# Reordering a weight conversion and two sets of channel sums in a fused attention and MLP kernel

## The chip, the cores and the metric

The kernel runs on one core of one Trainium2 chip. The metric is the device time of one execution in microseconds (us), the median of several runs. The engines of the core are TensorE (PE in the profile, its weight loads PEld), VectorE (DVE), ScalarE (ACT), GpSimd (POOL) and SyncE (SP, which here only issues DMAs). Each works through its own instructions in order and waits for others by semaphores.

## The reference

```python
def _attn_ref(q, k, v, S1, S2):                      # q, k, v: (4, 4, 1088, 32), S1, S2: (8, 32)
    def phi(x):
        a = np.einsum('rd,bhsd->bhsr', S1, x)
        b = np.einsum('rd,bhsd->bhsr', S2, x)
        return np.einsum('bhsi,bhsj->bhsij', a, b).reshape(*x.shape[:-1], r * r)
    q_p, k_p = (phi(q), phi(k))
    kv = np.einsum('bhsf,bhsd->bhfd', k_p, v)
    z = np.sum(k_p, axis=2)
    num = np.einsum('bhsf,bhfd->bhsd', q_p, kv)
    den = np.einsum('bhsf,bhf->bhs', q_p, z)[..., None] + 1e-06
    return num / den

# x: (4352, 128) = attention output as tokens by channels; w_in (128, 2048), w_out (2048, 128)
h = x @ w_in
g = 0.5 * h * (1.0 + erf(h / sqrt(2)))
out = g @ w_out
```

A linear attention with features of 64 values for each head is followed by an MLP with an exact gelu. S1, S2, w_in and w_out arrive as 64-bit floating-point numbers, and the engines work on 32-bit ones, so the kernel converts them itself.

## The kernel before

**Tiles and steps.** The 4352 tokens are cut into eight chunks of 512 and a ninth of the remaining 256. The hidden width of 2048 is cut into 16 tiles of 128 (`NF`). A step `t` is one pair (chunk, tile): `hidden` multiplies the weight tile by the chunk's tokens into PSUM (L740, two matmul passes) and ACT takes the gelu (L747). The steps go: t = 0 to 3 are tiles 0 to 3 of chunk 0, t = 4 to 11 tiles 0 to 7 of chunk 1, t = 12 to 23 the rest of chunk 0, t = 24 to 31 the rest of chunk 1, and then chunk after chunk.

**Two ways to multiply by w_out.** The first four tiles of chunk 0 and the first eight of chunk 1 are multiplied directly (`project`, L925). All others go by a scheme of seven products in place of eight. Four hidden tiles make a block (`NB`). For each block POOL forms four sums of gelu results, `token_sums` (L791 to L794, into the tiles bits_low, bits_a, bits_e and bits_m, four operations on 128x512), right after the block's last gelu. For each piece of w_out POOL once forms four sums of weights, `channel_sums` (L778 to L781, into the `small` tiles). `two_products` (L826) multiplies them on PE some steps later. The first products of a block are "4" and "7", which need the channel sums of the piece and the block's first token sum, bits_low. Block 1 of chunk 0 (t = 12 to 15) uses piece 2 of w_out, block 2 (t = 16 to 19) piece 3, block 3 (t = 20 to 23) piece 4. The products of block 1 begin in step 19, those of block 2 in step 22, those of block 3 in step 26.

**The weight pieces.** w_in and w_out are cut into five pieces each, two of 256 and three of 512. Pieces 0 and 1 are converted before the steps and in the first of them. Pieces 2, 3 and 4 are the six "turns", in the order w_in 2, w_out 2, w_in 3, w_out 3, w_in 4, w_out 4. A conversion (`Rounding`) of one piece has seven operations on 128x512:

- on DVE by `begin`: the exponent field (L283) and the mantissa field (L288);
- on ACT by `by_scalar`: the low words (`low_words`, L270) and the exponents (`exponents`, L294, which needs L283);
- on DVE by `end`: mantissas (L302, needs the low words), signs (L307, needs the exponents), and the product that writes the weights (L312). For some pieces the product goes to POOL instead (`multiply`).

`begin` of a turn stands ahead of `end` of the turn before it, so DVE's order is fields of the next piece, then mantissas, signs and product of this one.

**Order.** `at(t, f, ...)` puts a function in the list `slots[t]`. In a step the loop issues `hidden`, then the token sums, then the functions of the slot in the order in which `at` named them, then the products. In step 4, `first_hidden` and the products stand ahead of `hidden`. At the end every engine's instructions are tied to the order of the text, so no scheduler moves them.

**What follows the turns.** At t = 13 DVE turns the keys of batch 1 (`key_turn_blocks`, L383, two tiles kT), at t = 15 the queries of chunk 2 (L554). At t = 16 PE multiplies the turned keys (`features_of_all`, L1043, sixteen small matmuls, eight for each kT), then turns the remaining keys (L348); at t = 17 it uses those (L421). DVE makes features of the keys (L1051 to L1058) and sums them over tokens (L1067). On POOL, `widen_v_rem` (L364, L366) copies the remaining values of batch 1 when they have landed.

The SP queue issues all loads and most stores; the loads of the pieces, then of the later batches, are issued in one list before the steps.

Of the kernel before, what the change touches and what calls it, by code (L numbers as in the profile page):

```python
# [16 lines left out]
def kernel(  # L17
# [18 lines left out]
    pe, dve, act, pool, sp = nc.tensor, nc.vector, nc.scalar, nc.gpsimd, nc.sync  # L36
# [31 lines left out]
    def work_banks():  # L68

        return wps.tile([128, 2, CW], FP, name="w_ps")  # L70

    def work_bank():
        return work_banks()[:, 0]

    def halves(banks):
        return [banks[:, i] for i in range(2)]

    def hidden_bank():
        return hps.tile([128, CW], FP, name="h_ps")
# [494 lines left out]
    def expand_copy(n, i):  # L574
        A[i] = att.tile([128, 2, CW // 2], FP, name="A_sb")
        act.copy(out=A[i][:, :, :width[n] // 2], in_=B_of[n, i][:, :, :width[n] // 2])

    def expand_multiply(n, i):
        W = width[n]
        a, b = (t.rearrange("f g (r x) -> f g r x", r=2) for t in (A[i][:, :, :W // 2], B_of[n, i][:, :, W // 2:W]))  # L580
        dve.tensor_mul(out=qp[n].rearrange("f r (g x) -> f g r x", g=G)[:, 2 * i:2 * i + 2], in0=a, in1=b)
# [96 lines left out]
    def numerators_by_token(n, banks, tokens):  # L678

        for at, i in enumerate(tokens):  # L680
            to = by_head(banks[at // 2]).rearrange("p (j c r) x -> p j r c x", j=2, c=NP)[:, at % 2]
            for r in range(2):
                for half in range(2):
                    rows, tok = slice(half * 64, (half + 1) * 64), i * 128 + half * 64
                    pe.matmul(to[rows, r], lhsT=qp[n][:, r, tok:tok + 64], rhs=kz_apart[:, r], start=True, stop=True)
# [5 lines left out]
    def divide(n, banks, first, den=None):  # L691

        if den is None:
            den = att.tile([128, NP, 2 * H], FP, name="den_tok")
            for i, bank in enumerate(banks):
                dve.tensor_scalar(out=den[:, i], in0=by_head(bank)[:, :, D], scalar1=1e-6, scalar2=None, op0=AX.add)
        den = den[:, :len(banks)]
        dve.reciprocal(out=den, in_=den)
        for i, bank in enumerate(banks):
            dve.tensor_mul(out=x_half(n, first + i).rearrange("p j h d -> p (j h) d"), in0=by_head(bank)[:, :, 0:D],  # L700
                           in1=den[:, i, :, None].broadcast_to([128, 2 * H, D]))
# [25 lines left out]
    def w_tile(w, fi):  # L727
        i = max(i for i, (c0, c1) in enumerate(pieces) if c0 <= fi * 128)
        at = fi * 128 - CUTS[i]
        return w[i][:, at:at + 128]  # L730
# [3 lines left out]
    def hidden(n, fi, by_halves=False):  # L734
        W = width[n]
        ps = first_banks.pop((n, fi)) if (n, fi) in first_banks else hidden_bank()
        w = w_tile(w_in_sb, fi)
        for rows in (slice(0, 64), slice(64, 128)) if by_halves else (slice(0, 128),):
            if (n, fi) not in begun:
                pe.matmul(ps[rows, :W], lhsT=w[:, rows], rhs=xT[n][:, :W], start=True, stop=True)  # L740
        if n < NCH and fi < USUAL[n]:
            g_of[n, fi] = mlp.tile([128, CW], FP, name="g", bufs=4)
        else:
            if fi % NB == 0:
                blocks[n, fi // NB] = block(FP)
            g_of[n, fi] = blocks[n, fi // NB][:, fi % NB]
        act.activation(out=g_of[n, fi][:, :W], in_=ps[:, :W], func=ACT.Gelu)  # L747

    def first_hidden(n, half):

        if half == 0:
            first_banks[n, 0] = hidden_bank()
        parts = 1 if n else 2
        for i in range(parts):
            cols = slice(half * 256 + i * 256 // parts, half * 256 + (i + 1) * 256 // parts)
            pe.matmul(first_banks[n, 0][:, cols], lhsT=w_tile(w_in_sb, 0), rhs=xT[n][:, cols], start=True, stop=True)  # L756
# [53 lines left out]
    def first_block(n):  # L810
        return USUAL[n] // NB if n < NCH else 0
# [102 lines left out]
    def project(n, fi, parts=range(B // 2), cols=slice(None)):  # L914
        first, final = fi == (BLOCKED if n == NMAIN else 0), fi == (USUAL[n] if n < NCH else NF) - 1
        if first and n not in o_of:
            o_of[n] = out_bank() if n < NMAIN else [out_bank() for i in range(B // 2)]
        g = g_of[n, fi]
        if n == NMAIN:

            for i in parts:
                pe.matmul(o_of[n][i][:, :128], lhsT=g[:, i * 128:(i + 1) * 128], rhs=w_tile(w_out_sb, fi),  # L922
                          start=first, stop=final)
            return
        pe.matmul(o_of[n][:, cols], lhsT=w_tile(w_out_sb, fi), rhs=g[:, cols], start=first, stop=final)  # L925
# [107 lines left out]
    def at(t, f, *a):  # L1033
        slots[t].append(lambda: f(*a))
# [90 lines left out]
    def begin(w):  # L1125

        rounding[w.name] = Rounding(w)
        rounding[w.name].fields()

    def by_scalar(w, *what):  # L1130
        for f in what:
            getattr(rounding[w.name], f)()
# [10 lines left out]

    turns = [w[i] for i in range(2, 5) for w in (w_in_sb, w_out_sb)]
    both, low, exp = ("low_words", "exponents"), ("low_words",), ("exponents",)
    at(4, begin, turns[0])
    for k, acts in enumerate((((4, both),), ((5, low), (6, exp)), ((7, both),), ((8, low), (9, exp)), ((10, both),),
                              ((11, low), (12, exp)))):
        if k + 1 < len(turns):
            at(acts[-1][0], begin, turns[k + 1])  # L1150
        for t, what in acts:
            at(t, by_scalar, turns[k], *what)
        at(acts[-1][0], end, turns[k], dve if k < 4 else pool)
    at(12, channel_sums, 3)
    at(12, widen_v_rem, 1)
    at(12, multiply, turns[4])
    at(13, multiply, turns[5])
    for r in range(2):
        at(13, key_turn_blocks, 1, r)
    at(15, query_turn, 2)  # L1160
# [11 lines left out]
    at(24, query_sketch, 2)  # L1172
    at(26, lambda: turn_kv(1, held["kv"]))
    at(24, query_outer, 2)
    for i, t in enumerate((5, 6, 8)):
        at(t, channel_sums, i)
    at(6, spread_sketches)
    at(40, repeat_first_z)
    for n in range(3, NCHUNK):

        t = (n - 1) * NF
# [75 lines left out]
    for t in range(len(steps) + LAG):  # L1257
        if t < 4:

            hidden(0, t)  # L1260
            if t == 0:
                expand_multiply(1, 0)
                w_out[0].fields()
                expand_copy(1, 1)
                expand_multiply(1, 1)
            if t == 1:
                w_out[0].low_words()
                w_out[0].exponents()
                w_out[0].finish()
                w_out[1].fields()  # L1270
            if t == 2:
                w_out[1].low_words()
            if t == 3:
                banks = work_banks()
                numerators_by_token(1, halves(banks), range(JC))
                w_out[1].mantissas(by_pool=True)
                w_out[1].exponents()
                divide(1, halves(banks), 0)
                w_out[1].signs()
                w_out[1].product()  # L1280
                project(0, 0)
                project(0, 1, cols=slice(0, 256))
                turn_half(1, 0, work_bank(), by_act)
                project(0, 1, cols=slice(256, 512))
                turn_half(1, 1, work_bank(), by_dve)
            continue
        if t == 4:
            first_hidden(1, 0)
            for f, *a in products[t]:
                f(*a)  # L1290
            first_hidden(1, 1)
        for n in drains[t]:
            drain(n)
        sooner = t == NMAIN * NF
        if sooner:
            for f, *a in products[t]:
                f(*a)
        if t < len(steps):
            n, fi = steps[t]
            hidden(n, fi, by_halves=t >= 18)  # L1300
        if t < len(steps) and steps[t][0] < NMAIN and steps[t][1] % NB == NB - 1:
            n, b = steps[t][0], steps[t][1] // NB
            if b >= first_block(n):
                token_sums(n, b)
        for f in slots[t]:
            f()
        for n in done[t]:
            store(n)
        if t != 4 and not sooner:
            for f, *a in products[t]:  # L1310
                f(*a)
# [41 lines left out]
```

## Time and profile before

| | |
|---|---|
| runs | 258.88, 258.69, 258.60 us; median 258.69 |
| profiled execution | 258.58 us, its span 256.7 us |
| PE | 252.0 us busy (98% of the span), granted clock 1.00 |
| DVE | 158.1 us busy (62%) |
| ACT | 114.2 us busy (44%) |
| POOL | 180.1 us busy (70%) |
| chain that ended last | PE 91%, DVE 6%, issue 1%, ACT 1% |

The profile is of one execution. The span runs from its first to its last instruction, and all positions below are microseconds from the span's start. A row of a timeline gives start, length, engine, line, operation, tiles and shapes, and in brackets how long the engine was idle before it and which instruction ended that. Rows of one engine overlap slightly, as instructions are pipelined; the distance from start to start is what an instruction costs its engine. The chain that ended last is followed back from the last instruction: at each step to what released it.

### The profile page before, as it was taken

Reading aid. Unit: us, or ns where it says so; the run is one execution under the profiler, and the core shown is the slowest. Engines: PE = TensorE matmul, PEld = TensorE weight load, DVE = VectorE, ACT = ScalarE, POOL = GpSimd, SP = SyncE. Lnnn points to the kernel's source line nnn. Section 1 sums busy time; section 2 is a strip of 40 time slices with the busy share of each in tenths; the row PEclk is TensorE's granted clock in tenths of the full one; section 3 lists DMA queues with packets and bytes.
Section 4 is the critical chain, followed back from the end, with each engine's and each line's share of the span. In section 5 each row is a group of like instructions: output and inputs, shape, how many; then the busy total and the mean of one; then the engine's idle time right before and its main releaser. Section 6 shows DMA issues by size and latency. Waiting matters only on the chain.

```text
span 256.7 us, 5996 instructions
## 1 busy us (share of the span) xinstructions
PE 252.0 (98%) x2427; PEld 132.8 (52%) x2427; DVE 158.1 (62%) x330; ACT 114.2 (44%) x221; POOL 180.1 (70%) x195
## 2 busy tenths in 40 slices
PE   8999999999999999999999999999999999999995
PEld 4755443455444545444444455455444444445784
DVE  4898999939798996580178986399307000700382
ACT  3784883433535333533335332533444333533541
POOL 3419548996858777587758775787758777877950
PEclk9999999999999999999999999999999999999999
DMA  6689558710001101102000002000200200020021
GB/s 209 201 284 315 150 117 217 195 18 8 0 3 15 26 4 20 23 10 33 3 0 0 0 13 35 0 4 0 40 4 4 40 1 3 5 36 3 0 35 31
DMA packets 29083, 13.50 MB, mean 53 GB/s; under 512 B 21888, under 2 KB 27264, under 8 KB 29056
## 3 DMA queue, kind: packets, MB, share of 16 engines
q1 hardware_dynamic: 28624, 12.79, 20.1%
q8 instruction: 19, 0.31, 0.5%
q10 hardware_dynamic: 432, 0.33, 0.4%
q14 instruction: 8, 0.07, 0.1%
HBM read 10.88 MB, written 2.23 MB: 51 GB/s over the span
## 4 chain that ended last, share of the span: by engine, by line
PE 91%; DVE 6%; issue 1%; ACT 1%; POOL 0%; DVEq 0%; ACTq 0%
PE h_ps L740 41%; PE o_ps L826 35%; DVE bits_e L307 2%; PE w_ps L896 2%; PE w_ps L456 1%; DVE bits_m L302 1%; PE w_ps L604 1%; PE w_ps L659 1%; PE w_ps L957 1%; PE o_ps L925 1%; PE w_ps L570 1%; PE w_ps L1043 1%; PE o_ps L922 1%; PE h_ps L756 1%; DVE bits_a L288 1%; PE h_ps L348 1%
## 5 line engine op out<-in xcount | busy, mean ns | idle before, releaser
L740 PE MATMUL h_ps<-xT,w_in 128*64 128x512 f32 (+2 forms) x536 | 137.2, 567 | 0.0
L747 ACT ACTIVATE block<-h_ps 128x512 f32<-128x512 f32 (+1 forms) x132 | 75.4, 572 | 119.1 <-PE h_ps L740 117.2
L826 PE MATMUL o_ps<-block,w_out 128*64 128x256 f32 x232 | 59.5, 379 | 0.0
L791 POOL TENSOR_TENSOR bits_low<-block 128x512 f32<-128x512 f32 x29 | 37.2, 1283 | 29.2 <-ACT block L747 29.2
L740 PEld LDWEIGHTS h_ps<-xT,w_in 128*64 128x64 f32 (+1 forms) x536 | 40.9, 140 | 26.9 <-issue 8.7
L826 PEld LDWEIGHTS o_ps<-block,w_out 128*64 128x64 f32 x232 | 31.7, 137 | 39.2 <-issue 28.3
L792 POOL TENSOR_TENSOR bits_a<-block 128x512 f32<-128x512 f32 x29 | 37.0, 1276 | 12.5 <-ACT block L747 12.5
L841 DVE COPY sums<-o_ps 64x256 f32<-64x256 f32 x8 | 3.3, 417 | 60.2 <-PE o_ps L826 60.2
L793 POOL TENSOR_TENSOR bits_e<-bits_a,block 128x512 f32<-128x512 f32 x29 | 37.3, 1288 | 2.3
L794 POOL TENSOR_TENSOR bits_m<-block,bits_e 128x512 f32<-128x512 f32 x29 | 37.1, 1279 | 2.3
L826 PE MATMUL o_ps<-block,small 128*64 128x256 f32 x116 | 29.8, 379 | 0.0
L826 PE MATMUL o_ps<-bits_low,small 128*64 128x256 f32 x116 | 29.8, 379 | 0.0
L826 PE MATMUL o_ps<-bits_a,small 128*64 128x256 f32 x116 | 29.8, 379 | 0.0
L826 PE MATMUL o_ps<-bits_m,w_out 128*64 128x256 f32 x116 | 29.8, 379 | 0.0
L826 PEld LDWEIGHTS o_ps<-block,small 128*64 128x64 f32 x116 | 15.7, 137 | 18.6 <-issue 11.4
L826 PE MATMUL o_ps<-bits_e,small 128*64 128x256 f32 x116 | 17.7, 383 | 0.0
L826 PEld LDWEIGHTS o_ps<-bits_m,w_out 128*64 128x64 f32 x116 | 15.9, 137 | 0.0
L826 PEld LDWEIGHTS o_ps<-bits_a,small 128*64 128x64 f32 x116 | 15.8, 137 | 0.0
L826 PEld LDWEIGHTS o_ps<-bits_low,small 128*64 128x64 f32 x116 | 15.7, 137 | 0.0
L616 DVE STREAM_TRANSPOSE w_ps<-w_ps 128x512 f32<-128x512 f32 (+1 forms) x7 | 4.8, 687 | 17.1 <-ACT xT L670 12.7
L826 PEld LDWEIGHTS o_ps<-bits_e,small 128*64 128x64 f32 x116 | 7.9, 137 | 11.4 <-issue 9.8
L925 PE MATMUL o_ps<-g,w_out 128*128 128x512 f32 (+1 forms) x26 | 12.4, 563 | 0.0
(223 smaller groups left out, 322.0 us busy)
## 6 DMA issues: line engine op xcount, KB each, us to landing
block<-in_moe_w_in_dram SPq DMA_DIRECT2D x3, 512.0 KB, 8.8
block<-in_moe_w_out_dram SPq DMA_DIRECT2D x3, 512.0 KB, 10.5
k<-in_k_dram SPq DMA_DIRECT2D x12, 128.0 KB, 3.1
v<-in_v_dram SPq DMA_DIRECT2D x12, 128.0 KB, 3.4
q<-in_q_dram SPq DMA_DIRECT2D x24, 64.0 KB, 2.6
out_dram<-oT SPq DMA_DIRECT2D x21, 64.0 KB, 2.2
q_first<-in_q_dram SPq DMA_DIRECT2D x2, 256.0 KB, 3.9
v<-in_v_dram SPq DMA_DIRECT2D x2, 256.0 KB, 4.4
```

Source lines behind the costliest of these rows:

```text
L307: dve.scalar_tensor_tensor(out=self.e, in0=self.hi, scalar=0x80000000, in1=self.r, op0=AX.bitwise_and, op1=AX.bitwise_or)
L616: dve.transpose(out=tok, in_=ps[:, :, :H2])
L740: pe.matmul(ps[rows, :W], lhsT=w[:, rows], rhs=xT[n][:, :W], start=True, stop=True)
L747: act.activation(out=g_of[n, fi][:, :W], in_=ps[:, :W], func=ACT.Gelu)
L791: pool.tensor_sub(out=s[3], in0=a11, in1=a21)
L792: pool.tensor_add(out=s[1], in0=a21, in1=a22)
L793: pool.tensor_sub(out=s[2], in0=s[1], in1=a11)
L794: pool.tensor_sub(out=s[4], in0=a12, in1=s[2])
L826: pe.matmul(acc[n][bank][half * 64:(half + 1) * 64, col:col + HW], lhsT=fixed, rhs=moving, start=opens and e == 0 and name in "4715", stop ...
L841: dve.tensor_copy(out=N[lo, 0, one], in_=a0[lo, one])
L896: pe.matmul(acc[NMAIN][rows, COLS_REM[name]], lhsT=tokens[:, rows], rhs=fixed, start=k == 0 and name == ORDER_REM[0], stop=k == BLOCKED // ...
L925: pe.matmul(o_of[n][:, cols], lhsT=w_tile(w_out_sb, fi), rhs=g[:, cols], start=first, stop=final)
```

## The change

The first turn (w_in 2) is begun, and its two ACT operations are issued, in step 4 ahead of `first_hidden` of chunk 1 and so ahead of that chunk's first gelu; before, ACT did them behind that gelu. The product of w_in 4 goes from POOL to DVE. The channel sums of w_out 2 go from t = 8 to t = 14 and those of w_out 3 from t = 12 to t = 16; those of w_out 0, 1 and 4 stay at 5, 6 and 18. POOL's order after the spreading of the sketches becomes: copy of the remaining values, product of w_out 4, channel sums of w_out 2, token sums of block 1, channel sums of w_out 3, channel sums of w_out 4, token sums of block 2. Before, it was: channel sums of w_out 2, of w_out 3, copy of the remaining values, products of w_in 4 and w_out 4, token sums of block 1, channel sums of w_out 4, token sums of block 2. PE's order is the same, DVE's has the one product more, and no DMA is added or moved.

```diff
     turns = [w[i] for i in range(2, 5) for w in (w_in_sb, w_out_sb)]
     both, low, exp = ("low_words", "exponents"), ("low_words",), ("exponents",)
-    at(4, begin, turns[0])
-    for k, acts in enumerate((((4, both),), ((5, low), (6, exp)), ((7, both),), ((8, low), (9, exp)), ((10, both),),
-                              ((11, low), (12, exp)))):
+    schedule = ((), ((5, low), (6, exp)), ((7, both),), ((8, low), (9, exp)), ((10, both),), ((11, low), (12, exp)))
+    for k, acts in enumerate(schedule):
+        t1 = acts[-1][0] if acts else 4
         if k + 1 < len(turns):
-            at(acts[-1][0], begin, turns[k + 1])
+            at(t1, begin, turns[k + 1])
         for t, what in acts:
             at(t, by_scalar, turns[k], *what)
-        at(acts[-1][0], end, turns[k], dve if k < 4 else pool)
-    at(12, channel_sums, 3)
+        at(t1, end, turns[k], dve if k < 5 else pool)
     at(12, widen_v_rem, 1)
-    at(12, multiply, turns[4])
     at(13, multiply, turns[5])
+    for i, t in enumerate((5, 6, 14)):
+        at(t, channel_sums, i)
+    at(16, channel_sums, 3)
     for r in range(2):
         at(13, key_turn_blocks, 1, r)
...
-    for i, t in enumerate((5, 6, 8)):
-        at(t, channel_sums, i)
     at(6, spread_sketches)
...
         if t == 4:
+            begin(turns[0])
+            by_scalar(turns[0], *both)
             first_hidden(1, 0)
             for f, *a in products[t]:
                 f(*a)
```

## The prediction

> **What bounds the kernel now.** I read the page first, then the chain of waits, then the timelines of the engines from 20 to 60 us.
>
> ```profile
> PE 252.0 (98%) x2427; PEld 132.8 (52%) x2427; DVE 158.1 (62%) x330; ACT 114.2 (44%) x221; POOL 180.1 (70%) x195
> ```
>
> PE is busy 98% of the span, so only idle time of PE can be won. The chain that ended last leaves PE for long in one place, from 23.3 to 41.7 us:
>
> ```profile
> 38.15 0.86 DVE bits_m L302
> 39.01 1.96 DVE bits_e L307
> 40.97 0.63 DVE kT L383
> 41.60 0.14 issue
> 41.73 1.14 PE w_ps L1043 x16
> ```
>
> There DVE converts the six weight pieces and only then turns the keys (L383), for which PE waits. The timeline of PE gives the loss, that of DVE and ACT what made DVE late:
>
> ```profile
> 40.31 1.02 PE L740 MATMUL h_ps<-xT,w_in 128*128 128x512 f32 x2
> 41.73 1.14 PE L1043 MATMUL w_ps<-kT,S_ab 64*32 64x256 f32 x16 [0.40 <-DVE kT L383]
> 42.80 0.33 PE L348 MATMUL w_ps<-ident,k_rem 128*128 128x128 f32 x1
> 68.47 0.64 PE L1043 MATMUL w_ps<-kT,S_ab 64*32 64x256 f32 x16
> 23.41 0.60 ACT L747 ACTIVATE g<-h_ps 128x512 f32<-128x512 f32 x1 [2.14 <-PE h_ps L756]
> 23.90 0.67 ACT L270 ACTIVATE bits_low<-block 128x512 f32<-128x512 uint32 x1
> 24.60 0.75 DVE L302 SCALAR_TENSOR_TENSOR bits_m<-bits_a,bits_low 128x512 f32<-128x512 uint32 x1 [0.91 <-ACT bits_low L270]
> ...
> 34.08 0.68 DVE L307 SCALAR_TENSOR_TENSOR bits_e<-block,bits_r 128x512 uint32<-128x512 uint32 x1
> ...
> 38.93 2.04 DVE L307 SCALAR_TENSOR_TENSOR bits_e<-block,bits_r 128x512 uint32<-128x512 uint32 x1
> 40.89 1.29 DVE L383 STREAM_TRANSPOSE kT<-k 128x512 f32<-128x512 f32 x2
> ```
>
> Three things hold DVE up: 0.91 us idle for ACT at 24.60; rows of 0.94 instead of 0.68 us wherever POOL's channel sums run beside them; and the last L307, 2.04 instead of 0.68, beside POOL's product of w_in 4 (39.12, 1.29 us).
>
> **What PE can win.** L740 pairs start 0.86 apart, so after 40.31 the next start is 41.17, and 0.10 later for narrow tiles (54.04 to 55.00 is 0.96): 41.27. It came at 41.73, 0.46 late. The sixteen L1043 took until 42.80, 1.07, as the second half waited for the second kT; at 68.47 the same sixteen took until 69.04, 0.57. That is 0.50 more. Together 0.96 us. From there PE starts without a pause.
>
> **DVE after the change.** The first piece's low words and exponents go on ACT behind its copy of 20.89. Low words start at about 21.3. Exponents wait for L283 (21.89 to 22.31) and start at 22.35; ACT is free some 0.61 later, before the gelu that PE releases at 23.41. So I cost the move at nothing; the cover is ACT's 2.14 us idle ahead of that gelu, and without it the gelu would slip by 0.3 to 1.2 us. DVE's first L302 can start at 23.61 instead of 24.60. The gelus after it are paced by PE (27.64, 31.07 and 32.79 each waited for L740), so ACT's later conversions hardly move: the second piece's exponents end near 27.13 (the gelu two steps on waits for L740 of 24.86 and starts at 25.92, plus 0.48, plus 0.73). Its L307 starts there, at 27.17, instead of 27.95.
>
> From one L307 to the next, undisturbed rows (32.81 to 35.40) give 0.71 to the product, 0.61, then 0.34 and 0.34 for L283 and L288, and 0.60: 2.60 us. Channel sums no longer run beside them, as those of w_out 2 and 3 move behind. Three more pieces: 34.97. Then the product (0.71), which the change adds to DVE for w_in 4, 0.61 more, and 0.60 to the last L307: 36.89, ending at 37.57. ACT's last exponents end at 36.76, just in time. So a DVE product of some 0.6 us is added, and a wait of 0.91, a block of 1.36 and some 1.4 us of disturbed rows go.
>
> One disturbance is new: POOL, now with an empty queue, copies v_rem (L366) as soon as it lands. That load is issued at 32.96 and takes 2.3, so the copy starts at 35.3, beside DVE's L307 and the new product. A product beside a channel sum took 0.83 (32.06) instead of 0.69: 0.14. By the other rows it is between 0 and 0.48, the copy's whole length. I take 0.14, the row of the same operation: the last L307 ends at 37.71. The key turns end near 39.0, 2 us before PE asks at 41.27, so the whole 0.96 is free to be won.
>
> The Trainium skill ("SBUF — State Buffer", Who interferes with whom) says that a DVE instruction with two SBUF inputs and a GpSimd instruction that reads SBUF exclude each other for a whole instruction. The trace agrees at 38.93 (1.36 lost beside a 1.29 us product). By that rule the copy would cost its whole 0.48 instead of 0.14.
>
> **POOL after the change.** This is what is late next. POOL does, in order: product of w_out 4, channel sums of w_out 2, token sums of block 1, channel sums of w_out 3, of w_out 4, token sums of block 2. Durations are those of the rows below, start to start:
>
> ```profile
> 41.04 1.30 POOL L312 TENSOR_TENSOR w_out<-bits_m,bits_e 128x512 f32<-128x512 f32 x1 [0.63 <-DVE bits_e L307]
> 42.30 1.27 POOL L791 TENSOR_TENSOR bits_low<-block 128x512 f32<-128x512 f32 x1
> ...
> 47.48 0.46 POOL L778 TENSOR_TENSOR small<-w_out 128x128 f32<-128x128 f32 x1
> ...
> 49.26 1.28 POOL L791 TENSOR_TENSOR bits_low<-block 128x512 f32<-128x512 f32 x1
> 51.46 0.38 PE L826 MATMUL o_ps<-bits_low,small 128*64 128x256 f32 x1
> ```
>
> Product 1.26, token sums 5.18, channel sums 1.78 each. After 37.71 and 0.08 for the release: 37.79, 39.05 (channel sums of w_out 2), 40.83 (block 1; its last gelu ends at 40.25, so that doesn't bind), 46.01, 47.79, 49.57 (block 2), and its first sum is there at 50.85, with 0.08 for the release 50.93. Before, block 2 began at 49.26: earlier, although POOL's product ended later, since one set of channel sums stood ahead of it then and two stand there now.
>
> PE wants this sum at 51.46 less 0.96, 50.50. So PE stalls 0.43 us there. Block 1's sums are wanted at 44.9 and there at 42.1; block 2's second sum is wanted at 52.6 and there at 52.1; block 3 has over 3 us. Nothing else of PE's order moves, no DMA is moved or added, and the stall is not made up later, as PE is full.
>
> Sum: 0.96 - 0.43 = 0.53 us. The profiled execution took 258.58 (span 256.7 and 1.9 around it): 258.05. The median of the runs shown is 258.69, 0.11 above it: **258.15 us**. A difference of 0.2% (0.52 us) is about what a measurement of this kernel can tell from none, so the forecast lies on that edge.
>
> **Rivals.**
> - *POOL is no limit.* If the copy costs nothing, DVE runs ahead a little and the stalled products cost PE less than the wait, the full 0.96 is won: 257.7. For it: POOL could start block 1 as early as 40.3 (the gelu), where the stall is gone. Against it: this needs DVE's last L307 to end 0.5 sooner than added up. Chance 0.20.
> - *The copy blocks DVE for its whole length.* Then the stall is 0.43 + 0.34 = 0.77 and 0.19 is left: 258.5. For it: the 2.04 us row. Against it: rows beside single channel sums lost only 0.14 to 0.27. This is also the result by the Trainium skill's rule above. Chance 0.18.
> - *Slower: channel sums meet DVE operations that hold them up.* At 29.43 a set took 2.90 (to 32.34) beside L302 and L307, instead of 1.78. The set of w_out 3 at 46.0 now stands between the two blocks of token sums; if it takes 2.90, the stall grows by 1.12 to 1.55, and PE loses 0.59: 259.3. It decides from 0.53 us of added delay on. Against it: DVE then runs the reductions L1067, and the set of w_out 4 took 0.46 a row beside just these (47.48 to 49.26). Chance 0.06.
> - *The gelu slips* behind the moved conversion. PE needs its bank for the hidden product at 24.86, so 0.85 us of slip is free; for 0.3 more the gain falls to about 0.2. Chance 0.02.
>
> **How the numbers follow.** The forecast has 0.54, with a range of its own of 257.95 to 258.35 (the copy from 0 to 0.3 us, and 0.1 for each release and step). About half of it lies beyond 0.2%. Faster: 0.29 of it and the 0.20 of the first rival, 0.49. Same: 0.25, 0.18 and 0.02, 0.45. Slower: 0.06. The range reaches from the full gain to nearly none, 257.65 to 258.60.
>
> **What would show it.** In the profile of the changed kernel: L270 and L294 ahead of the gelu near 23.4 and no idle of DVE near 24; no L307 over 1 us; L383 before 39.5; L1043 near 41.27 with no idle before it and L348 some 0.57 after. On POOL, block 2's first L791 at 49.6. On PE, an idle of about 0.4 us near 50.5 ahead of L826 with bits_low, released by POOL. It is wrong if L1043 still waits for kT, if POOL's block 2 begins by 49.2 or after 50, or if PE idles elsewhere by over 0.1 us.

## The result and the profile after

The changed kernel takes 258.05 us (median of 17 runs), the kernel before 258.69 us in the runs beside it. The ratio is 0.9975, with a 95% interval from 0.9967 to 0.9983: faster by 0.25%, a little beyond the 0.2% that was called measurable. The forecast was 258.15 us, on that edge. The ratios here and below leave out single runs that were far slower (such as 267.57 us here and 441.24 us in e4_sums4_twice), while the medians are of all runs.

The profiled execution of the changed kernel has a span of 255.9 us. Everything in it lies 0.28 us earlier than in the profile of before, from ahead of the first step on: PE's last L740 pair before the key products starts at 40.03 instead of 40.31, with nothing different on PE in between. This differs from execution to execution (below), so distances are taken from that L740 pair.

The timeline of PE after the change, at the key turn and at block 2's first products:

```profile
40.03 1.02 PE L740 MATMUL h_ps<-xT,w_in 128*128 128x512 f32 x2
40.98 0.66 PE L1043 MATMUL w_ps<-kT,S_ab 64*32 64x256 f32 x16
41.57 0.33 PE L348 MATMUL w_ps<-ident,k_rem 128*128 128x128 f32 x1
...
50.22 0.59 PE L826 MATMUL o_ps<-block,small 128*64 128x256 f32 x2
50.59 0.43 PE L826 MATMUL o_ps<-bits_low,small 128*64 128x256 f32 x1
50.65 0.38 PE L826 MATMUL o_ps<-block,small 128*64 128x256 f32 x1
```

L1043 now follows L740 without idle time, and the sixteen of them take 0.59 us. L348 stands 1.54 after the L740 pair instead of 2.49: PE won 0.95 us. Then comes what was not there before: the first product with bits_low stands 0.37 behind its neighbour from the `small` tile, where before it stood 0.01 behind. The waits show who held it:

```profile
PEld o_ps L826 <- POOL bits_low L791: 0.6, 2, 0.4
```

(Engine and line that waited, whom it waited for, total, times, longest.) The timelines of ACT and DVE, and of POOL, answer to the rest of the steps:

```profile
20.88 0.69 ACT L270 ACTIVATE bits_low<-block 128x512 f32<-128x512 uint32 x1
22.11 0.72 ACT L294 ACTIVATE bits_r<-bits_e,below 128x512 uint32<-128x512 uint32 x1 [0.55 <-DVE bits_e L283]
23.06 0.60 ACT L747 ACTIVATE g<-h_ps 128x512 f32<-128x512 f32 x1 [0.22 <-PE h_ps L756]
...
23.32 0.81 DVE L302 SCALAR_TENSOR_TENSOR bits_m<-bits_a,bits_low 128x512 f32<-128x512 uint32 x1
...
35.40 0.69 DVE L312 TENSOR_TENSOR w_in<-bits_m,bits_e 128x512 f32<-128x512 f32 x1
36.01 0.78 DVE L302 SCALAR_TENSOR_TENSOR bits_m<-bits_a,bits_low 128x512 f32<-128x512 uint32 x1
36.71 0.68 DVE L307 SCALAR_TENSOR_TENSOR bits_e<-block,bits_r 128x512 uint32<-128x512 uint32 x1
37.31 1.29 DVE L383 STREAM_TRANSPOSE kT<-k 128x512 f32<-128x512 f32 x2
```

```profile
35.82 0.42 POOL L366 COPY v_rem_aug<-v_rem 64x128 f32<-64x128 f32 x1 [8.01 <-DMA v_rem<-in_v_dram]
37.47 1.33 POOL L312 TENSOR_TENSOR w_out<-bits_m,bits_e 128x512 f32<-128x512 f32 x1 [1.23 <-DVE bits_e L307]
40.52 1.28 POOL L791 TENSOR_TENSOR bits_low<-block 128x512 f32<-128x512 f32 x1
...
45.70 0.45 POOL L778 TENSOR_TENSOR small<-w_out 128x128 f32<-128x128 f32 x1
...
47.48 0.46 POOL L778 TENSOR_TENSOR small<-w_out 128x128 f32<-128x128 f32 x1
...
49.26 1.28 POOL L791 TENSOR_TENSOR bits_low<-block 128x512 f32<-128x512 f32 x1
```

ACT converts ahead of the gelu and still waits 0.22 us for PE before it. DVE no longer idles near 24, no L307 is longer than 0.69 us, and the key turns start at 37.31 and end at 38.60, 2.4 us before PE uses them. On POOL two sets of channel sums stand between block 1's and block 2's token sums, and block 2 begins at 49.26: the same moment as before, while PE is 1.23 us ahead of where it was (0.28 of it the early start).

Where block 3's first product with bits_low starts (60.18 before, 59.36 after), both shifts are in: 19.87 us after the L740 pair before, 19.33 after. The change is worth 0.54 us in the traces, 0.95 won and 0.41 given back.

### The profile page after: what moved, and what is told of

Its sections match the earlier page's. It is cut to its first block, busy times and chain, and to the rows that moved or that the text cites. A ratio compares the mean times of both kernels' runs of the same rounds, so it can differ in the third digit from the quotient of the medians.

```text
span 255.9 us, 5994 instructions
## 1 busy us (share of the span) xinstructions
PE 251.8 (98%) x2427; PEld 132.7 (52%) x2427; DVE 156.9 (61%) x331; ACT 114.6 (45%) x221; POOL 177.6 (69%) x194
## 4 chain that ended last, share of the span: by engine, by line
PE 98%; ACT 0%; DVE 0%; issue 0%
PE h_ps L740 45%; PE o_ps L826 35%; PE o_ps L925 4%; PE w_ps L896 2%; PE w_ps L456 1%; PE w_ps L604 1%; PE w_ps L659 1%; PE w_ps L957 1%; PE w_ps L570 1%; PE o_ps L922 1%; PE h_ps L756 1%; PE o_ps L445 1%; PE w_ps L1043 1%; PE h_ps L348 1%; PE w_ps L685 0%; PE o_ps L397 0%
## 5 line engine op out<-in xcount | busy, mean ns | idle before, releaser
L740 PE MATMUL h_ps<-xT,w_in 128*64 128x512 f32 (+2 forms) x536 | 138.0, 567 | 0.0
L791 POOL TENSOR_TENSOR bits_low<-block 128x512 f32<-128x512 f32 x29 | 37.2, 1281 | 28.4 <-ACT block L747 28.4
L740 PEld LDWEIGHTS h_ps<-xT,w_in 128*64 128x64 f32 (+1 forms) x536 | 41.4, 140 | 26.9 <-issue 8.4
```

The source lines that it names most:

```text
L791: pool.tensor_sub(out=s[3], in0=a11, in1=a21)
```

## The experiments

Theory A, from the prediction: PE can win 0.96 us at the key turn, whatever brings the keys early enough, and the changed kernel loses 0.4 of it because POOL has two sets of channel sums ahead of block 2's first token sum. Theory B has two forms: that the loss near 50.5 is PE's own, or that the channel sums must leave DVE's stretch before the wait goes. Theory C is on the placing: that it does not matter where the product of w_in 4 is done, and that keeping the channel sums clear of DVE is what brings the gain.

All numbers of the traces in this table are distances in us. "L348" and "block 3" (its first product with bits_low) are counted from the start of the L740 pair ahead of L1043, "stall" is the start of block 2's first product with bits_low less that of its neighbour, and "gain" is block 3's distance before less the kernel's own. "Time" is the median, with the ratio to the kernel before in runs beside it.

| kernel | L348 | stall | block 3 | gain | time | ratio (95%) |
|---|---|---|---|---|---|---|
| before | 2.49 | 0.01 | 19.87 | | 258.69 | |
| after | 1.54 | 0.37 | 19.33 | 0.54 | 258.05 | 0.9975 (0.9967 to 0.9983) |
| e1_act_first | 1.69 | 0.01 | 19.07 | 0.80 | 257.72 | 0.9963 (0.9950 to 0.9975) |
| e2_rest | 1.55 | 1.21 | 20.18 | -0.31 | 258.92 | 1.0012 (1.0003 to 1.0022) |
| e3_sums4_late | 1.55 | 0.01 | 18.92 | 0.95 | 257.38 | 0.9948 (0.9937 to 0.9960) |
| e4_sums4_twice | 1.55 | 2.13 | 21.10 | -1.23 | 260.01 | 1.0056 (1.0035 to 1.0077) |
| e5_product_pool | 1.54 | 1.02 | 19.99 | -0.12 | 258.74 | 1.0005 (0.9994 to 1.0015) |
| e6_sums2_early | 1.54 | 0.00 | 18.92 | 0.95 | 257.40 | 0.9953 (0.9941 to 0.9965) |
| e7_sums3_early | 1.54 | 0.30 | 19.26 | 0.61 | 257.87 | 0.9970 (0.9958 to 0.9982) |
| e8_copy_late | 1.55 | 0.26 | 19.23 | 0.64 | 258.42, one run | |

**One part alone: e1_act_first.** The kernel before, with only the ACT operations of the first piece moved ahead of the gelu.

```diff
-    at(4, begin, turns[0])
-    for k, acts in enumerate((((4, both),), ((5, low), (6, exp)), ...
+    for k, acts in enumerate((((4, ()),), ((5, low), (6, exp)), ...
...
         if t == 4:
+            begin(turns[0])
+            by_scalar(turns[0], *both)
             first_hidden(1, 0)
```

> The kernel before with one part of the change only: the first piece's ACT operations ahead of chunk 1's first gelu. Products and channel sums stay where they were. Theory A (PE can win 0.96 us at the key turn and no more, and what the changed kernel gave back, 0.45 us, it lost because two sets of channel sums stood ahead of block 2's first token sum): DVE and the first kT come 0.78 us earlier, 40.8 instead of 41.6, the second at 41.4, so L1043 starts at 41.27 and hardly waits; on POOL one set of channel sums stands between blocks 1 and 2, block 2 begins at 48.5, so no stall near 50.5: 0.9 us faster than before, 257.75. Theory B (the channel sums and the product must leave DVE's stretch for the wait to go): the wait shrinks by half at most, 258.2 to 258.4.

Measured: 257.72 us, ratio 0.9963. The timelines of DVE and PE:

```profile
38.52 2.00 DVE L307 SCALAR_TENSOR_TENSOR bits_e<-block,bits_r 128x512 uint32<-128x512 uint32 x1
40.44 1.29 DVE L383 STREAM_TRANSPOSE kT<-k 128x512 f32<-128x512 f32 x2
...
40.66 1.02 PE L740 MATMUL h_ps<-xT,w_in 128*128 128x512 f32 x2
41.62 0.81 PE L1043 MATMUL w_ps<-kT,S_ab 64*32 64x256 f32 x16
42.35 0.33 PE L348 MATMUL w_ps<-ident,k_rem 128*128 128x128 f32 x1
```

DVE is disturbed as before, its last L307 still takes 2.00 us, and yet the first kT is there in time; only the second half of L1043 waits, 0.15 us. There is no stall at block 2. So this one part is enough for 0.80 us; added to it, the rest of the change brings the last 0.15 at the key turn and costs 0.41 further on. The form of theory B that wants the channel sums moved falls.

**The other parts alone: e2_rest.** The changed kernel without that part.

```diff
+    at(4, begin, turns[0])
-    schedule = ((), ((5, low), (6, exp)), ...
+    schedule = (((4, both),), ((5, low), (6, exp)), ...
...
         if t == 4:
-            begin(turns[0])
-            by_scalar(turns[0], *both)
```

> The changed kernel without that part: ACT converts the first piece behind the gelu again, the rest of the change stays. Theory A: DVE idles 0.9 us near 24 again, the key turns come 0.78 us later, near 38.3, still 3 us before PE asks, so PE wins its 0.96; but the last product, and with it POOL's whole queue up to block 2, comes 0.78 us later, so PE stalls about 1.2 us near 50.5: 0.25 us slower than before, 258.9. Theory B (the loss near 50.5 is PE's own, not POOL's): as the changed kernel, 258.05.

Measured: 258.92 us, ratio 1.0012, slower than before by some 0.1%, near theory A's 258.9 and far from theory B's 258.05. On PE:

```profile
50.34 0.59 PE L826 MATMUL o_ps<-block,small 128*64 128x256 f32 x2
51.55 0.43 PE L826 MATMUL o_ps<-bits_low,small 128*64 128x256 f32 x1 [0.61 <-POOL bits_low L791]
```

The wait for the keys is gone here too, so either part alone removes it (e1 all but 0.15 us); but POOL's last product comes at 38.45, and block 2's sums start at 50.22 instead of 49.26. The stall is 1.21 us.

**The suspected cost taken away: e3_sums4_late.**

```diff
-    at(18, channel_sums, 4)
+    at(20, channel_sums, 4)
```

> The changed kernel with the channel sums of w_out 4 at t = 20 instead of 18, so behind block 2's token sums. Theory A: block 2 begins 1.78 us earlier, its first sum is there near 49.1, the stall near 50.5 is gone and the two halves of PE stay in step: 0.96 us faster than before, 257.7. Theory B (the loss is PE's own): 258.05.

Measured: 257.38 us, ratio 0.9948. On POOL and PE:

```profile
45.66 0.46 POOL L778 TENSOR_TENSOR small<-w_out 128x128 f32<-128x128 f32 x1
47.44 1.28 POOL L791 TENSOR_TENSOR bits_low<-block 128x512 f32<-128x512 f32 x1
...
50.19 0.38 PE L826 MATMUL o_ps<-block,small 128*64 128x256 f32 x1
50.20 0.38 PE L826 MATMUL o_ps<-bits_low,small 128*64 128x256 f32 x1
```

With one set of channel sums less ahead of it, block 2 begins 1.8 us sooner, the two products start together, and the whole 0.95 us stays won. The loss was POOL's order and nothing of PE's own. This kernel beats both.

**The suspected cost doubled: e4_sums4_twice.** The same sums are formed twice.

```diff
-    at(18, channel_sums, 4)
+    for i in range(2):
+        at(18, channel_sums, 4)
```

> The changed kernel with the channel sums of w_out 4 computed twice in a row at t = 18, the same values. Theory A: POOL's queue bounds PE there with slope one, so the stall grows by the whole 1.78 us to about 2.2, and the time is 1.78 above the changed kernel: 259.8, 1.1 us slower than before. Theory B: 258.05.

Measured: 260.01 us, ratio 1.0056; the wait on PE:

```profile
52.86 0.43 PE L826 MATMUL o_ps<-bits_low,small 128*64 128x256 f32 x1 [1.53 <-POOL bits_low L791]
```

The stall grew from 0.37 to 2.13 us, by 1.76 for 1.78 us more of POOL's time: slope one.

**The product: e5_product_pool.**

```diff
-        at(t1, end, turns[k], dve if k < 5 else pool)
+        at(t1, end, turns[k], dve if k < 4 else pool)
     at(12, widen_v_rem, 1)
+    at(12, multiply, turns[4])
```

> The changed kernel with the product of w_in 4 on POOL again. Theory A (POOL's queue up to block 2's first sum sets the loss): POOL's product reads beside DVE's last L302 and L307, which it holds up by some 1.3 us, DVE saves the 0.6 of its own product, so the product of w_out 4 and all behind it on POOL comes 0.7 us later; L1043 still does not wait; the stall near 50.5 grows from 0.4 to 1.1: 0.7 above the changed kernel, 258.75, about the time before. Theory C (where the product is done does not matter, as DVE has 3 us to spare at the key turn): 258.05.

Measured: 258.74 us, ratio 1.0005, no different from before. The timeline of DVE:

```profile
36.49 1.54 DVE L307 SCALAR_TENSOR_TENSOR bits_e<-block,bits_r 128x512 uint32<-128x512 uint32 x1 [0.40 <-ACT bits_r L294]
37.95 1.29 DVE L383 STREAM_TRANSPOSE kT<-k 128x512 f32<-128x512 f32 x2
```

The keys are still early: the second turn ends at 39.24, and PE starts L1043 at 40.96. The last L307 takes 1.54 instead of 0.68 us beside POOL's product, and DVE waits 0.40 for ACT, which its own product had covered. Together the last product and block 1 come 0.65 later from the L740 pair (41.15 less 40.01, against 40.52 less 40.03), and the stall grows by just that, to 1.02. The expected 1.3 us of blocking was 0.86 and a wait; the sum held. So theory C falls for the product: its place matters, through POOL and not through the keys.

**The channel sums moved back, one set at a time: e6_sums2_early and e7_sums3_early.**

```diff
-    for i, t in enumerate((5, 6, 14)):
+    for i, t in enumerate((5, 6, 8)):
```

> The changed kernel with the channel sums of w_out 2 at t = 8 again. Theory A: DVE is disturbed for 0.7 us beside them, which it can spare; POOL's product ends near 39.4 and block 1 begins as soon as its last gelu allows, 0.47 sooner than in the changed kernel; the stall of 0.36 us near 50.2 goes: 0.4 below the changed kernel, 257.65. Theory C (keeping the channel sums clear of DVE is what brings the gain): 258.3 or more.

Measured: 257.40 us, ratio 0.9953, no stall. Block 1 begins at 39.70 and block 2 at 48.43. Counted from the L740 pair (40.06 here) block 1 begins 0.85 us sooner than in the changed kernel, not 0.47: it was expected to wait for the block's last gelu, which runs from 39.40 to 40.00 here, but the first token sum (L791) reads only the first and third tile of the block.

```diff
-    at(16, channel_sums, 3)
+    at(12, channel_sums, 3)
```

> The changed kernel with the channel sums of w_out 3 at t = 12 again. Theory A: they start behind the copy of the remaining values near 36.2 and run beside DVE's last two operations, 0.5 us disturbed, and ahead of the last product, so block 1 begins 0.7 later, but one set less stands ahead of block 2, which begins 1.1 us sooner: no stall, 257.65. Theory C: 258.3 or more.

Measured: 257.87 us, ratio 0.9970. Here a stall of 0.30 was left where none was expected:

```profile
37.41 0.54 POOL L366 COPY v_rem_aug<-v_rem 64x128 f32<-64x128 f32 x1 [9.09 <-DMA v_rem<-in_v_dram]
37.92 0.45 POOL L778 TENSOR_TENSOR small<-w_out 128x128 f32<-128x128 f32 x1
39.70 1.29 POOL L312 TENSOR_TENSOR w_out<-bits_m,bits_e 128x512 f32<-128x512 f32 x1
```

In this execution, whose 258.18 us lie above the median, SP issued the load of the remaining values only at 34.93 (33.55 in the profile after), the copy waited for it until 37.41, and the channel sums of w_out 3 stood in POOL's queue behind the copy. They did not start at 36.2 as counted, but at 37.92, and pushed the product to 39.70. Whether the stall would be gone with an earlier load was not tried. Theory C falls for the sums in both cases: moving either set back is no worse than the changed kernel, and for w_out 2 it is clearly better.

**The disturbing copy moved away: e8_copy_late.**

```diff
-    at(12, widen_v_rem, 1)
+    at(20, widen_v_rem, 1)
```

> The changed kernel with the copy of the remaining values at t = 20, off DVE's stretch. If the copy holds DVE up by what the changed kernel's trace shows (the L302 at 36.0 takes 0.70 from start to start instead of 0.60), that row is back at 0.60, the last product and block 1 come 0.10 sooner, and the stall near 50.5 is 0.1 shorter, 0.26 instead of 0.36. If the copy cost DVE its whole length, 0.4.

Measured in one run: the last L302 takes 0.60 us from start to start, and the stall is 0.26. The copy cost DVE 0.10 us, and the stall follows by 0.11. The single time (258.42 us) tells nothing at this size.

## Why the prediction was right

Point by point, with 0.28 us added to the positions of the profile after, to count from the same moment:

- **PE's win, 0.96.** It is 0.95, and the same in all of e2 to e8, however early the keys were. The two parts of it, the wait ahead of L1043 and the wait inside, both showed: e1 leaves only the second, 0.15.
- **ACT at no cost.** Low words at 21.16 (forecast 21.3), exponents at 22.39 (22.35), and 0.22 us of idle left ahead of the gelu.
- **DVE's count.** The last L307 ends at 37.67 (37.71). The row-by-row count of 2.60 us a piece held.
- **The copy, 0.14.** It is 0.10 (e8). It fell on the L302 at 36.01, not on the product, as SP issued the load at 33.55, where 32.96 was counted. The prediction's 0.48, "the copy's whole length", already contains a wait for DVE: alone the copy takes 0.28 (e8, at 55.30). In these profiles, between 28 and 41 us, the two engines take turns. Wherever an L302, L307 or L312 of DVE was lengthened beside POOL, it ended 0.54 to 0.56 after POOL's operation, and wherever the copy was lengthened (0.42 to 0.61), it ended 0.14 or 0.15 after DVE's. So it was here: the copy began beside the L312 at 35.40 and ended at 36.24, 0.15 after it; the L302 ended at 36.79, 0.55 after the copy. The copy costs DVE only what is left of it when DVE's next operation is ready. As an estimate from these distances, that is at most 0.28 + 0.55 - 0.68 = 0.15; it was nothing in e5 and e7, where none of the three was ready behind it. So 0.14 was near the right size by luck: it was taken from another pair of operations. The second rival falls.
- **The exclusion behind it.** The rule of the Trainium skill ("SBUF — State Buffer", Who interferes with whom) that a DVE instruction with two SBUF inputs and a GpSimd one that reads SBUF exclude each other for a whole instruction agrees with these distances. Only the price of 0.48 that the prediction drew from it does not. The 128x512 products on POOL fit as well: L307 lost 1.36 us in the kernel before and 0.86 in e5, and ended 0.56 after the product in both (38.93 + 2.04 against 39.12 + 1.29, and 36.49 + 1.54 against 36.20 + 1.27). The 1.36 is not the product's alone, as L307 started while the copy still ran. On POOL, before:

```profile
38.67 0.48 POOL L366 COPY v_rem_aug<-v_rem 64x128 f32<-64x128 f32 x1
39.12 1.29 POOL L312 TENSOR_TENSOR w_in<-bits_m,bits_e 128x512 f32<-128x512 f32 x1
```

- **POOL's queue.** Block 1 at 40.80 (40.83), block 2 at 49.54 (49.57), the stall 0.37 (0.43). Half of the 0.06 is this shift of 0.03, half the release, which takes 0.05 us, not 0.08.
- **What was missed.** After the stall 0.04 to 0.06 us more is lost by block 3, in every kernel with a stall (table: block 3 less stall is 18.96 to 18.97 there, 18.92 without). In the trace the two halves of PE's columns run out of step after the stall: the first operation of the next hidden product stands alone at 51.08 and the other three at 51.50. That would account for it, but was not tried by itself.
- **The rivals.** That POOL is no limit is refuted: with the copy away (e8) only 0.10 more is won. Its earliest start for block 1, 40.3 with the last gelu, was read wrongly (e6), which changes nothing here. The slower rival, channel sums held up beside DVE, did not come: those of w_out 3 took 0.45 each beside the reductions. Its price was right in kind, as e4 shows with added work in the same place.

The forecast by the traces was 0.53 and it is 0.54. The mechanism was right, but so close a match is luck in part: the stall was counted 0.06 too long, and the 0.04 lost after it was not counted at all. (The sum written down comes to 258.16, not 258.15.) The medians differ by 0.64, and those of e3 and e6 by 1.2 to 1.4 where the traces show 0.95. In the profiled executions the rest lies ahead of the steps: PE's first L740 starts between 14.79 and 15.55 us in these profiles, at 15.11 in that of before and at 14.79 and 14.86 in e3 and e6. What sets this was not tried, and one profile of each kernel does not show whether the medians differ for the same reason.

## What to carry to other kernels

When a wait on the bound engine is removed, count its next need of every other engine from the new, earlier moment: here the queue that had 0.9 us to spare was 0.4 us too late once PE came 0.95 us sooner and the queue, with one more item ahead, 0.28 us later (both counted from the L740 pair). Once the late producer has slack, further relief to it is worth nothing, and work moved out of its way is not free where it lands; each of the two parts removed the wait alone (all but 0.15 us of it in e1), and one of them gave more than both together. A queue's order near a deadline can be tested cheaply by doing one item twice: a slope of one shows that it is on the path.

## What the runs showed of the hardware that was not expected

- The load of the remaining values (32 KB) ended POOL's wait anywhere from 35.6 to 37.4 us in seven profiles of almost the same program. What differs is when SP issued it; the wait ended 2.3 to 2.5 us behind that (33.22 and 35.63 in e5, 33.55 and 35.82 after, 34.52 and 36.92 in e2, 34.93 and 37.34 in e6, 34.93 and 37.41 in e7). e5 and e6 reach the key turn within 0.05 us of each other, so this is not a later start of the whole; what held SP up was not tried. Work queued behind such a wait inherits the spread, as e7 did.
- What a DVE operation with two SBUF inputs lost beside POOL, 0.10 us beside a copy of 64x128, about 0.26 beside each 128x128 sum, and 0.86 to 1.36 beside a 128x512 product, was not a share of POOL's length: between 28 and 41 us it ended 0.54 to 0.56 after POOL's operation each time, so the loss follows from what was left of that operation.
- An operation of DVE that already waited was passed over when POOL's next one followed without a gap: L307 started at 38.93 during the copy, and the product that started at 39.12 went first (in e1 likewise, 38.52 and 38.71).
